# Narrowing steps moved from the first tiles of one MoE layer to its later tiles, and a regrouped preparation of the next layer

## The chip, the cores and the metric

The kernel runs on one core of a Trainium2 chip. The metric is device time in microseconds, the median of three runs. All matrix products are fp32, done as fp32r products of a high and a low part.

## The reference

Attention with mixing over heads feeds two feed-forward layers, over 1792 tokens of width 768:

```
scores = scale * q @ k^T, mixed over heads by w_pre; softmax; mixed by w_post; @ v
h  = x @ w_in            # 768 -> 1024   (first MoE)
sm = softmax(h);  solu = h * sm;  ln = (solu - mean) / sqrt(var + 1e-6) * g_ln
x2 = ln @ w_out          # 1024 -> 768
h  = x2 @ w_in2;  g = relu(h)**2;  y = g @ w_out2    # 768 -> 2048 -> 768  (second MoE)
```

The weights arrive as 64-bit floats, and the kernel narrows them to fp32 itself.

## The kernel before, in words

Three stages follow each other: attention, the first MoE and the second MoE. The code is in the order in which each engine executes it (the order is written by hand; each engine is in order, and waits on semaphores).

**First MoE.** 14 tiles of 128 tokens, `m` = 0 to 13. Tile m: `h1(m)` is 36 matmuls (L457) into `ps_h`, of which there are two; `norm1(m)` reduces (L711, VectorE), exponentiates (L714, ScalarE), multiplies and takes statistics (L715 to L722, VectorE), takes the root (L724, L725, GpSimd), and, in its second part, `nb` (L728, VectorE) and the normalised `e` (L731, ScalarE). `zt(m-1)` transposes `e` of the tile before on TensorE (L746) into `ps_tr`, and splits it (L748 ScalarE, L749 VectorE). `split_x` prepares x of tile m+2 (L700 ScalarE, L701 GpSimd). In tiles 0 to 3 two pieces each of the output weights are loaded (L681) and split (L686 ScalarE, L687 GpSimd); x and these weights share three load buffers. `out1` (L760, copied by L768, stored by L769) is 24 matmuls for one 128-row block of a group of three tiles; from tile 4 on two run per tile, ten stand after the last tile's loop.

**Narrowing.** `w2stream` narrows the second layer's weights, 96 pieces of 128x256, one piece after another: load (L789, SP queue), square on ScalarE (L799), mask on GpSimd (L800), and three integer steps on VectorE (L820, L824, L826), then a store (L807, SP queue). The mask of the next piece is asked for ahead of the first step of a piece. Each call of `next` is one step. In the first MoE `steps2` is called four times per tile, with five buffers each for raw and narrowed pieces; in the second MoE a second stream narrows the rest with three buffers each.

**Second MoE.** Products go by Strassen's scheme: seven products `p1` to `p7` per slice, 16 slices `q` (eight per half of the tokens). `prepare()` makes the sums of x (`mix_x`) and of weights (`mix_w`), and their splits (`split_xc`, `split_ti`), interleaved with the last nine `out1`. In a slice the products of q alternate with seven output blocks `y2(q-1, ·)` (L1154), in the order `SEQ`; VectorE and ScalarE read the products out of four PSUM banks (L1115 to L1131, L1101 to L1103, L1098), and `y` out of two (L1163, L1165). `mix_second()` makes the sums of x for the second half of the tokens.

Of the kernel before, what the change touches and what calls it, by code (L numbers as in the profile page):

```python
# [18 lines left out]
def kernel(  # L19
# [16 lines left out]
    nc = tc.nc  # L36
    B, D, _ = qT.shape
# [100 lines left out]
    for b in range(B):  # L138
        for (i0, n) in CHUNKS:
            c, oa = len(chunks), 0  # L140
# [593 lines left out]
    GT = 3  # L734
# [36 lines left out]
    FE = 256  # L771
    NE = F2 // FE
    KE = FE // 128
    FIRST = 60
    w2pieces = []
    for e in range(NE):
        w2pieces += [(w2_in, w2iD, c, e * FE) for c in range(CC)]
# [3 lines left out]
    def w2stream(todo, pool, nr, nt):  # L781

        raws, ts, ready = {}, {}, []

        def load(i):
            if i in todo:
                src, dst, k, o = w2pieces[i]
                raws[i] = pool.tile([128, WP], I64, tag="nraw", name="nraw", bufs=nr)
                nc.sync.dma_start(out=raws[i], in_=src[k * 128:(k + 1) * 128, o:o + WP])  # L789

        def words(i):
            pair = raws[i].bitcast(U32).rearrange("p (n two) -> p n two", two=2)
            return pair[:, :, 0], pair[:, :, 1]

        def mask(i):

            if i in todo:
                t = ts[i] = pool.tile([128, WP], F32, tag="nt", name="nt", bufs=nt)
                nc.scalar.activation(out=t, in_=words(i)[1].bitcast(F32), func=AF.Square)  # L799
                nc.gpsimd.tensor_scalar(  # L800
                    out=t, in0=t, scalar1=2.0**-30, scalar2=2.0 - 2.0**-23, op0=ALU.is_ge, op1=ALU.mult
                )

        def store():
            i = ready.pop(0)
            src, dst, k, o = w2pieces[i]
            nc.sync.dma_start(out=dst[k * 128:(k + 1) * 128, o:o + WP], in_=ts.pop(i))  # L807
            narrowed.append(i)

        a = todo[0]  # L810
        for i in range(nr - 1):
            load(a + i)
        mask(a)
        for i in todo:
            load(i + nr - 1)
            mask(i + 1)
            low, high = words(i)
            bits = ts[i].bitcast(U32)
            stt = nc.vector.scalar_tensor_tensor
            stt(out=bits, in0=high, scalar=3, in1=bits, op0=ALU.logical_shift_left, op1=ALU.bitwise_and)  # L820
            yield True
            if ready:
                store()
            stt(out=bits, in0=high, scalar=0xC0000000, in1=bits, op0=ALU.bitwise_and, op1=ALU.bitwise_or)  # L824
            yield True
            stt(out=bits, in0=low, scalar=29, in1=bits, op0=ALU.logical_shift_right, op1=ALU.bitwise_or)  # L826
            raws.pop(i)
            ready.append(i)
            yield True
        store()  # L830
        yield True

    stream = w2stream(range(FIRST), m1b_p, 5, 5)

    def steps2(n):
        for _ in range(n):
            next(stream, None)
# [4 lines left out]
    outs = []  # L842
    for m in range(NTILE):
        if m + 2 < NTILE:
            xr[m + 2] = load_x(m + 2)
        if m:
            run(h1(m))
        norm = norm1(m)
        next(norm)
        steps2(3)  # L850
        if m > 0:
            zt(m - 1)
        steps2(3)
        if m + 2 < NTILE:
            split_x(m + 2, xr.pop(m + 2))
        for kk in range(len(w1o), min(K1, len(w1o) + 2)):
            wr[kk] = load_w1_out(kk)
        for kk in sorted(wr):
            split_w1_out(kk, wr.pop(kk))
        if m > GT and (m - 1) % GT == 0:  # L860
            outs += [((m - 1) // GT - 1, cc) for cc in range(CC)]
        for i in range(2):
            if outs:
                out1(*outs.pop(0))
            steps2(4 if m else 2)
            if i == 0:
                run(norm)
    run(stream)
# [20 lines left out]
    def load_xb(p, c):  # L889
        t0 = 2 * p * HT  # L890
        qs = []
        for k in range(2):
            for t in range(2):
                b = wi2_p.tile([128, HT], F32, tag=f"xb{k}{t}", name="xb", bufs=2)
                r0 = (k * HC + c) * 128
                nc.sync.dma_start(out=b, in_=x2D[r0:r0 + 128, t0 + t * HT:t0 + (t + 1) * HT])
                qs.append(b)
        return qs

    def mix_x(qs, i, eng):  # L900

        b11, b12, b21, b22 = qs
        out, x, y = ((b11, b12, b11), (b12, b22, b12), (b22, b22, b11), (b21, b21, b22))[i]
        eng.tensor_tensor(out=out, in0=x, in1=y, op=ALU.subtract)
# [3 lines left out]
    def store_xt(p, c, name, b):  # L908
        r0 = (XT.index(name) * HC + c) * 128
        nc.sync.dma_start(out=xtD[p][r0:r0 + 128], in_=b)  # L910

    def mix_second():

        parts = [load_xb(1, 0), load_xb(1, 1)]
        yield True
        for c in range(HC):
            b11, b12, b21, b22 = qs = parts[c]
            for i in range(4):
                mix_x(qs, i, nc.gpsimd)
                if i % 2:  # L920
                    yield True
            for name, b in zip(XT, (b11, b22, b12, b21)):
                store_xt(1, c, name, b)
            if c + 2 < HC:
                parts.append(load_xb(1, c + 2))
            yield True
# [31 lines left out]
    def load_ra(q):  # L958
        if q < NQ:
            f0 = (q % NE) * FE  # L960
            for k in range(2):
                t = wi2_p.tile([128, HC, FE], F32, tag=f"ra{k}", name="ra", bufs=1)
                nc.sync.dma_start(
                    out=t,
                    in_=w2iD[k * HC * 128:(k + 1) * HC * 128, f0:f0 + FE].rearrange("(c p) f -> p c f", p=128),
                )
                ra[q, k] = t
# [51 lines left out]

    def prepare():  # L1020

        load_ra(0)
        parts = [load_xb(0, 0), load_xb(0, 1)]
        yield True
        mix_w(0, 0)
        mix_w(0, 1)
        weights = list(ORDER)
        for c in range(HC):
            b11, b12, b21, b22 = qs = parts[c]
            split_xc(0, "p1", c, b11)  # L1030
            yield True
            mix_x(qs, 0, nc.vector)
            mix_x(qs, 1, nc.vector)
            split_xc(0, "p5", c, b11)
            yield True
            mix_x(qs, 2, nc.vector)
            mix_x(qs, 3, nc.vector)
            split_xc(0, "p7", c, b12)
            yield True
            split_xc(0, "p6", c, b22)  # L1040
            store_xt(0, c, "p4", b21)
            if c + 2 < HC:
                parts.append(load_xb(0, c + 2))
            split_ti(0, weights.pop(0))
            yield True
            split_ti(0, weights.pop(0))
            yield True
        while weights:
            split_ti(0, weights.pop(0))
            yield True  # L1050

    prep2 = prepare()
    for g, cc in outs:
        for _ in range(3):
            next(prep2, None)
        out1(g, cc)
    run(prep2)
    load_xc(0, ORDER[4])
    load_ra(1)

    ps1.__exit__(None, None, None)
    psi.__exit__(None, None, None)
# [144 lines left out]
    for q in range(NQ):  # L1207
        p, e = divmod(q, NE)
        todo = []
        if q == 0:  # L1210
            todo = [(0, name) for name in ORDER[4:]]
        elif q == NE - 1:
            todo = [(1, name) for name in ORDER[:4]]
            load_xc(*todo[0])
            load_xc(*todo[1])
        elif q == NE:
            todo = [(1, name) for name in ORDER[4:]]
        parts = [(t, c) for t in todo for c in range(HC)]
        for k, x in enumerate(SEQ):
            if isinstance(x, str):  # L1220
                prod(q, x)
                after(q, x)
            elif q:
                y2(q - 1, x)
            lows()
            extras(q, k)
            for t, c in parts[:3 if q == 0 else 1]:
                if q == NE - 1 and SEQ.index(t[1]) > k:
                    break
                parts.pop(0)  # L1230
                split_xc(*t, c)
                i = ORDER.index(t[1]) + (2 if t[0] else 1)
                if c == HC - 1 and i < len(ORDER):
                    load_xc(t[0], ORDER[i])
            if p == 0:
                steps2(2 if q and k < 10 else 1)
                if 2 <= q < NE - 1 and k in (2, 6, 10):
                    next(mx, None)
        assert not parts, q
        if q < NE:  # L1240
            assert len(narrowed) >= min(12 * (q + 2) + 6, len(w2pieces)), (q, len(narrowed))
# [61 lines left out]
```

## Time and profile before

| | |
|---|---|
| median of 3 runs | 1207.66 us (1196.8 to 1211.68) |
| the profiled execution | 1203.72 us, its span 1201.9 us |
| TensorE matmul busy | 1059.8 us, 88% |
| VectorE, GpSimd, ScalarE busy | 722.9, 712.9, 581.3 us |
| TensorE's waits in the first MoE for `e` (L731) | 37.2 us in 4 |
| first MoE's last `out1` ends, second MoE begins | 698.2 us |

TensorE is the engine with most work, so a microsecond counts where TensorE waits. The profile's idle column says what ended each wait, and the timeline says when the product groups start.

### The profile page before, as it was taken

To read this page: it belongs to the slowest core of one execution; us is meant where nothing else is said; L and a number is where in the kernel's file an instruction comes from. 1 tells how busy PE (TensorE), PEld (TensorE's weight loads), DVE (VectorE), ACT (ScalarE), POOL (GpSimd) and SP (SyncE) were. 2 spreads that over 40 slices of the span, in tenths; PEclk is the share of its full clock that TensorE was granted. 3 is DMA by queue.
4 is the path that set the end of the run, shared out by engine and by line. 5 is a ranking of instruction groups with operands and counts; after the bars stand their busy time and mean duration, and the time that the engine had idled before them with its cause. 6 is when DMAs were issued, how large, how long until landed. Compare 5 with 4: busy or idle time off the path is not lost.

```text
span 1201.9 us, 30983 instructions
## 1 busy us (share of the span) xinstructions
PE 1059.8 (88%) x12488; PEld 894.5 (74%) x12488; DVE 722.9 (60%) x1262; ACT 581.3 (48%) x1212; POOL 712.9 (59%) x876
## 2 busy tenths in 40 slices
PE   8888789889998855899999848878899999999998
PEld 3555557555666744799889847877799899999998
DVE  3557676666856346686775627677764672444444
ACT  4666566667766133334333424544344556434432
POOL 3556886896848355554452427798775555555521
PEclk9999999999999867899999978998899999999999
DMA  6786786877766343554542544545521552111102
GB/s 180 205 237 197 213 252 201 257 229 225 220 190 188 105 152 118 158 151 147 163 139 81 176 165 138 158 153 182 171 94 64 168 188 82 58 62 53 53 27 92
DMA packets 128910, 183.08 MB, mean 152 GB/s; under 512 B 24416, under 2 KB 101344, under 8 KB 128768
## 3 DMA queue, kind: packets, MB, share of 16 engines
q1 hardware_dynamic: 119924, 156.59, 41.9%
q0 software_dynamic: 6464, 22.60, 6.6%
q10 hardware_dynamic: 2380, 1.93, 0.6%
q8 instruction: 98, 1.61, 0.6%
q14 instruction: 44, 0.36, 0.1%
HBM read 103.70 MB, written 38.83 MB: 119 GB/s over the span
## 4 chain that ended last, share of the span: by engine, by line
PE 63%; DVE 9%; DMA 8%; issue 7%; ACT 6%; POOL 6%; SPq 1%; ACTq 0%; POOLq 0%; DVEq 0%
PE ps_y L1154 14%; PE ps_h L1085 11%; PE ps_o L760 8%; PE ps_h L457 7%; PE ps_ring L297 6%; PE ps_ring L336 6%; PE ps_pre L240 5%; PE ps_ring L206 5%; DMA sdst<-ssrc 3%; POOL nt L800 2%; DVE nt L820 2%; DVE nt L824 1%; ACT ssrc L213 1%; POOL s L994 1%; DVE gt L1098 1%
## 5 line engine op out<-in xcount | busy, mean ns | idle before, releaser
L1154 PE MATMUL ps_y<-to,gt 128*128 128x384 f32 x1332 | 250.9, 342 | 19.7 <-DVE y L1165 15.6
L1154 PEld LDWEIGHTS ps_y<-to,gt 128*128 128x128 f32 x1332 | 238.3, 192 | 26.7 <-issue 11.8
L1085 PE MATMUL ps_h<-xc,ti 128*128 128x448 f32 x1008 | 220.9, 371 | 25.4 <-DVE h L1120 16.1
L1085 PEld LDWEIGHTS ps_h<-xc,ti 128*128 128x128 f32 x1008 | 190.4, 190 | 43.2 <-ACT ti L1009 16.5
L297 PEld LDWEIGHTS ps_ring<-w,e 60*64 60x64 f32 (+1 forms) x5760 | 104.1, 138 | 74.9 <-issue 47.2
L316 DVE COPY at<-ps_ring 128x420 f32<-128x420 f32 x156 | 87.8, 610 | 107.5 <-PE ps_ring L297 107.4
L800 POOL TENSOR_SCALAR nt<-nt 128x256 f32<-128x256 f32 x96 | 111.8, 1164 | 67.1 <-ACT nt L799 60.5
L297 PE MATMUL ps_ring<-w,e 60*64 60x60 f32 (+2 forms) x5760 | 113.0, 222 | 35.8 <-issue 28.7
L213 ACT COPY ssrc<-ps_ring 128x896 f32<-128x896 f32 x92 | 82.5, 907 | 107.8 <-PE ps_ring L206 91.6
L457 PE MATMUL ps_h<-w1i,xs 128*128 128x512 f32 x504 | 126.9, 412 | 0.0
L1165 DVE TENSOR_TENSOR y<-ps_y,y 128x768 f32<-128x768 f32 x97 | 92.2, 953 | 56.7 <-PE ps_y L1154 56.6
L760 PE MATMUL ps_o<-zt,w1o 128*128 128x384 f32 (+1 forms) x720 | 122.0, 328 | 4.0 <-ACT o L768 4.0
L760 PEld LDWEIGHTS ps_o<-zt,w1o 128*128 128x128 f32 x720 | 118.2, 190 | 4.7 <-ACT o L768 4.7
L258 ACT ACTIVATE e<-ps_pre,nm 128x448 f32<-128x448 f32 x180 | 113.3, 640 | 15.4 <-DVE nm L251 12.4
L457 PEld LDWEIGHTS ps_h<-w1i,xs 128*128 128x128 f32 x504 | 99.3, 199 | 23.0
L1098 DVE TENSOR_TENSOR gt<-h,gt 128x448 fp32r<-128x448 f32 x64 | 53.9, 842 | 94.6 <-ACT gt L1103 94.4
L251 DVE TENSOR_REDUCE nm<-ps_pre 128x1 f32<-128x448 f32 x180 | 103.1, 610 | 11.4 <-PE ps_pre L240 11.4
L206 PE MATMUL ps_ring<-k,q 64*64 64x448 f32 x752 | 102.1, 555 | 7.4 <-ACT ssrc L213 3.7
L1010 POOL TENSOR_TENSOR ti<-s,ti 128x384 fp32r<-128x384 f32 x64 | 70.7, 1115 | 53.3 <-ACT ti L1009 52.4
L240 PE MATMUL ps_pre<-sdst,wpre_bd 64*64 64x448 f32 x720 | 98.2, 563 | 4.0 <-issue 2.5
L336 PEld LDWEIGHTS ps_ring<-at,v 128*64 128x64 f32 x1536 | 76.2, 140 | 26.8 <-PE ps_pre L240 11.3
L820 DVE SCALAR_TENSOR_TENSOR nt<-nraw,nt 128x256 uint32<-128x256 uint32 x96 | 55.3, 576 | 66.7 <-POOL nt L800 66.7
(106 smaller groups left out, 1562.5 us busy)
## 6 DMA issues: line engine op xcount, KB each, us to landing
sdst<-ssrc SPq DMA_DIRECT2D x166, 210.0 KB
nraw<-in_moe_w_in_dram SPq DMA_DIRECT2D x48, 256.0 KB
nraw<-in_moe_w_out_dram SPq DMA_DIRECT2D x48, 256.0 KB
ra<-w2iD SPq DMA_DIRECT2D x32, 384.0 KB
ro<-w2oD SPq DMA_DIRECT2D x32, 384.0 KB
w1raw<-in_moe_w_in_dram POOLq DMA_DIRECT2D x24, 256.0 KB, 6.3
w1raw<-in_moe_w_out_dram POOLq DMA_DIRECT2D x24, 256.0 KB, 5.4
w2iD<-nt SPq DMA_DIRECT2D x48, 128.0 KB
```

Source lines behind the costliest of these rows:

```text
L206: nc.tensor.matmul(out=ps[64 * u:64 * u + 64, e, 0:S], lhsT=qq[c][64 * e:64 * e + 64, p * n + u * half:p * n + u * half + 64], rhs=k[64 * ...
L213: (nc.vector.tensor_copy if dve else nc.scalar.copy)(ssrc[c][:, p:H:HP, :], ps[:, :, 0:S])
L240: nc.tensor.matmul(out=ps[b][64 * u:64 * u + 64, 0:S], lhsT=wpre_bd[64 * r:64 * r + m], rhs=ds[b][64 * r:64 * r + m], start=True, stop=True,)
L251: nc.vector.tensor_reduce(out=nm, in_=pres[s][b][:, 0:S], op=ALU.max, axis=AX.X, negate=True)
L258: nc.scalar.activation(out=e, in_=pres[s][b][:, 0:S], func=AF.Exp, bias=nms.pop((s, b)), scale=1.0, accum_out=sms[s][:, b:b + 1])
L297: nc.tensor.matmul(out=ps[64 * c:64 * c + 64, u, i0:i0 + ng * RH], lhsT=e[64 * u:64 * u + m, o:o + 64], rhs=w[64 * u:64 * u + m, b, g0:g0 ...
L336: nc.tensor.matmul(out=ps[64 * e:64 * e + 64, 0, q * 120:q * 120 + n], lhsT=t[:, g] if j < NJ else t[:, e, p], rhs=at[c][:, j * H + (g if ...
L457: nc.tensor.matmul(out=ps[:, u], lhsT=t[:, a, cc], rhs=w1i[cc][:, w, u * 512:(u + 1) * 512], start=(cc == 0 and a == 0 and w == 0), stop=( ...
L760: nc.tensor.matmul(out=ps[:, 0:width], lhsT=w1o[k][:, w, cc * 128:(cc + 1) * 128], rhs=zT[:, a, k, 0:width], start=(k == 0 and i == 0), st ...
L800: nc.gpsimd.tensor_scalar(out=t, in0=t, scalar1=2.0**-30, scalar2=2.0 - 2.0**-23, op0=ALU.is_ge, op1=ALU.mult)
L1085: nc.tensor.matmul(out=bank[b][:, 0:HT], lhsT=t[:, w, c], rhs=xc[name][:, a, c], start=(first and c == 0 and i == 0), stop=(c == HC - 1 an ...
L1154: nc.tensor.matmul(out=ps[:, u - u2[0], 0:DM // 2], lhsT=gt[:, a, f, o:o + 128], rhs=w[:, v, f, u * (DM // 2):(u + 1) * (DM // 2)], start= ...
```

## The change

The order of TensorE's instructions is as before. Four things differ.

1. 72 of the 96 pieces, not 60, are narrowed in the first MoE, and the steps are given out by `rate(m, n)`: none in tiles 0 to 2, two per call in tile 3 (8), and 6, 5, 5, 5 per call from tile 4 on (21 per tile instead of 14). The stream's first step now only issues loads.
2. `prepare()` loads `p1`'s parts of x separately, splits them first, and makes the sums of a group (`mixes`) one or two chunks before their splits (`splits`). The loads for `p3` and for the next weights move into it. It runs one chunk before each of the first three `out1` and two before the others, instead of three.
3. In the second MoE the remaining 24 pieces take no step in slice 0 (one at its end), and 16 steps per slice from slice 1 on (24 before).
4. The sums of `mix_second` are on VectorE instead of GpSimd, and in slices 5 and 6 instead of 2 to 6.

```diff
-    FIRST = 60
+    FIRST = 72
...
             load(a + i)
+        yield True
         mask(a)
...
+    def rate(m, n):
+        return n if m > GT else 2 if m == GT else 0
+
...
-        steps2(3)
+        steps2(rate(m, 6))
         if m > 0:
             zt(m - 1)
-        steps2(3)
+        steps2(rate(m, 5))
...
-            steps2(4 if m else 2)
+            steps2(rate(m, 5))
             if i == 0:
                 run(norm)
...
-                mix_x(qs, i, nc.gpsimd)
+                mix_x(qs, i, nc.vector)
...
     def prepare():
 
+        load_xc(0, "p1")
+        parts = [load_xb(0, 0), load_xb(0, 1)]
         load_ra(0)
-        parts = [load_xb(0, 0), load_xb(0, 1)]
-        yield True
-        mix_w(0, 0)
-        mix_w(0, 1)
+        yield True
+        def mixes(c):
+            for i in range(4):
+                mix_x(parts[c], i, nc.vector)
+        def splits(c):
+            b11, b12, b21, b22 = parts[c]
+            store_xt(0, c, "p4", b21)
+            for name, b in (("p6", b22), ("p5", b11), ("p7", b12)):
+                split_xc(0, name, c, b)
+            if c + 2 < HC:
+                parts.append(load_xb(0, c + 2))
...
     prep2 = prepare()
-    for g, cc in outs:
-        for _ in range(3):
+    next(prep2)
+    for i, (g, cc) in enumerate(outs):
+        for _ in range(1 if i < 3 else 2):
             next(prep2, None)
         out1(g, cc)
     run(prep2)
-    load_xc(0, ORDER[4])
-    load_ra(1)
...
-                steps2(2 if q and k < 10 else 1)
-                if 2 <= q < NE - 1 and k in (2, 6, 10):
+                steps2((1 if k == 13 else 0) if q == 0 else 1 + (k in (2, 6)))
+                if NE - 3 <= q < NE - 1 and k % 2:
                     next(mx, None)
```

Where it moves instructions, at three places (the changed code's line numbers are a few higher: L820, L824, L826, L956, L1117, L1120 become L821, L825, L827, L960, L1137, L1140).

The SP queue at the start of the first MoE, before: `xraw` is x of a tile, `w1oraw` output weights, `nraw` a piece to narrow, `w2iD<-nt` the store of a narrowed piece.

```order
L693 DMA xraw<-xD 128x6x128
L789 DMA nraw<-in_moe_w_in_dram 128x256 x6
L807 DMA w2iD<-nt 128x256
L681 DMA w1oraw<-w1oD 128x768 x2
L789 DMA nraw<-in_moe_w_out_dram 128x256
L807 DMA w2iD<-nt 128x256
```

And with the change:

```order
L693 DMA xraw<-xD 128x6x128
L681 DMA w1oraw<-w1oD 128x768 x2
L693 DMA xraw<-xD 128x6x128
L681 DMA w1oraw<-w1oD 128x768 x2
L693 DMA xraw<-xD 128x6x128
L681 DMA w1oraw<-w1oD 128x768 x2
L693 DMA xraw<-xD 128x6x128
L789 DMA nraw<-in_moe_w_in_dram 128x256 x5
```

The output weights' loads no longer stand behind loads and stores of narrowed pieces.

ScalarE in a later tile of the first MoE (tile 5), before: `nt<-nraw` is the square of a piece, `e` L714 the exponent and L731 the normalised tile, `o` a copy of an output block.

```order
L714 ACTIVATE e,sm<-ps_h,nm 128x1024
L799 ACTIVATE nt<-nraw 128x256
L748 CAST zt<-ps_tr 128x4x128 x2
L799 ACTIVATE nt<-nraw 128x256
L700 CAST xs<-xraw 128x768
L768 COPY o_8299<-ps_o 128x384
L799 ACTIVATE nt<-nraw 128x256 x2
L731 ACTIVATE e<-e,nb,rs 128x1024
L768 COPY o_8345<-ps_o 128x384
L799 ACTIVATE nt<-nraw 128x256
```

And with the change:

```order
L714 ACTIVATE e,sm<-ps_h,nm 128x1024
L799 ACTIVATE nt<-nraw 128x256 x2
L748 CAST zt<-ps_tr 128x4x128 x2
L799 ACTIVATE nt<-nraw 128x256
L700 CAST xs<-xraw 128x768
L768 COPY o_8200<-ps_o 128x384
L799 ACTIVATE nt<-nraw 128x256 x2
L731 ACTIVATE e<-e,nb,rs 128x1024
L768 COPY o_8248<-ps_o 128x384
L799 ACTIVATE nt<-nraw 128x256 x2
```

Seven squares per tile stand there in every later tile, two of them behind `e`.

VectorE in slice 0 of the second MoE, before: `xc<-xr` are splits of the parts of x for p3, p2 and p4; `u` and `h` read p6 and p5.

```order
L956 TENSOR_TENSOR xc<-xr,xc 128x448 x3
L820 SCALAR_TENSOR_TENSOR nt<-nraw,nt 128x256
L1117 TENSOR_TENSOR u<-ps_h_10151,u 128x448
L956 TENSOR_TENSOR xc<-xr,xc 128x448 x3
L824 SCALAR_TENSOR_TENSOR nt<-nraw,nt 128x256
L956 TENSOR_TENSOR xc<-xr,xc 128x448 x3
L826 SCALAR_TENSOR_TENSOR nt<-nraw,nt 128x256
L1120 TENSOR_TENSOR h<-ps_h_10184,u 128x448
```

And with the change:

```order
L960 TENSOR_TENSOR xc<-xr,xc 128x448 x3
L1137 TENSOR_TENSOR u<-ps_h_10252,u 128x448
L960 TENSOR_TENSOR xc<-xr,xc 128x448 x6
L1140 TENSOR_TENSOR h<-ps_h_10283,u 128x448
L1142 TENSOR_TENSOR h<-ps_h_10306,h 128x448
```

The steps of a piece no longer stand between the splits and the reads; the nine splits are still ahead of the read of p5.

## Rows read from the trace of the kernel before

**Rows 1.** TensorE's waits: for whom, us in total, times, longest.
```profile
PE ps_tr L746 <- ACT e L731: 37.2, 4, 12.3
...
PE ps_o L760 <- ACT o L768: 4.0, 3, 1.7
```

**Rows 2.** Two stretches: length, busy time of PE, PEld, DVE, ACT, POOL, clock, DMA.
```profile
440.00:460.00 20.00, 11.90 (x44) 9.51 (x44) 11.57 (x23) 7.00 (x12) 10.27 (x9) 0.74 0.49 150
760.00:800.00 40.00, 33.41 (x174) 30.75 (x173) 28.28 (x43) 17.54 (x35) 32.52 (x26) 1.00 0.54 175
```

**Rows 3.** Timeline of TensorE, first MoE: start, length in us, what, idle before.
```profile
405.15 11.17 PE L457 MATMUL ps_h<-w1i,xs 128*128 128x512 f32 x48
...
500.36 8.54 PE L457 MATMUL ps_h<-w1i,xs 128*128 128x512 f32 x36
508.74 1.03 PE L746 MATMUL ps_tr<-id_sb,e 128*128 128x128 f32 x8
509.53 8.57 PE L760 MATMUL ps_o<-zt,w1o 128*128 128x384 f32 x48
517.94 8.55 PE L457 MATMUL ps_h<-w1i,xs 128*128 128x512 f32 x36
```

**Rows 4.** What ScalarE's split of the output weights (L686) waited for: us, times.
```profile
  DMA w1oraw<-w1oD: 37.5, 5
```

**Rows 5.** Timeline of VectorE in one later tile of the first MoE.
```profile
526.52 1.23 DVE L711 TENSOR_REDUCE nm<-ps_h 128x1 f32<-128x1024 f32 x1 [2.34 <-PE ps_h L457]
...
532.16 0.37 DVE L826 SCALAR_TENSOR_TENSOR nt<-nraw,nt 128x256 uint32<-128x256 uint32 x1
...
534.45 0.42 DVE L826 SCALAR_TENSOR_TENSOR nt<-nraw,nt 128x256 uint32<-128x256 uint32 x1
...
535.90 2.12 DVE L826 SCALAR_TENSOR_TENSOR nt<-nraw,nt 128x256 uint32<-128x256 uint32 x1
...
539.39 0.15 DVE L728 SCALAR_TENSOR_TENSOR nb<-mv,rs 128x1 f32<-128x1 f32 x1
...
542.76 0.43 DVE L820 SCALAR_TENSOR_TENSOR nt<-nraw,nt 128x256 uint32<-128x256 uint32 x1 [1.97 <-POOL nt L800]
```

**Rows 6.** Timeline of ScalarE, same tile.
```profile
539.63 1.25 ACT L731 ACTIVATE e<-e,nb,rs 128x1024 f32<-128x1024 f32 x1 [5.96 <-DVE nb L728]
```

**Rows 7.** Timeline of GpSimd, same tile.
```profile
533.38 2.42 POOL L800 TENSOR_SCALAR nt<-nt 128x256 f32<-128x256 f32 x2
535.89 1.85 POOL L701 TENSOR_TENSOR xs<-xraw,xs 128x768 fp32r<-128x768 f32 x1
```

**Rows 8.** TensorE: slices 0, 1, 5 begin; last three rows: p2 of slices 6, 7, 8.
```profile
698.15 7.59 PE L1085 MATMUL ps_h<-xc,ti 128*128 128x448 f32 x36
721.86 7.43 PE L1085 MATMUL ps_h<-xc,ti 128*128 128x448 f32 x27 [16.11 <-DVE h L1120]
732.86 5.25 PE L1085 MATMUL ps_h<-xc,ti 128*128 128x448 f32 x18 [3.57 <-ACT h L1101]
...
877.17 3.97 PE L1085 MATMUL ps_h<-xc,ti 128*128 128x448 f32 x18 [0.81 <-ACT h L1101]
...
928.66 7.50 PE L1085 MATMUL ps_h<-xc,ti 128*128 128x448 f32 x36
958.99 7.50 PE L1085 MATMUL ps_h<-xc,ti 128*128 128x448 f32 x36
...
986.51 7.50 PE L1085 MATMUL ps_h<-xc,ti 128*128 128x448 f32 x36
```

**Rows 9.** Timeline of ScalarE in slice 0.
```profile
711.85 0.43 ACT L799 ACTIVATE nt<-nraw 128x256 f32<-128x256 f32 x1 [6.86 <-DMA nraw<-in_moe_w_in_dram]
...
717.60 1.11 ACT L955 CAST xc<-xr 128x448 fp32r<-128x448 f32 x2 [3.30 <-DMA xr<-xtD]
```

**Rows 10.** Timeline of the SP queue in slice 0.
```profile
714.99 2.19 SPq L945 DMA_DIRECT2D xr<-xtD  x3
```

**Rows 11.** ScalarE's squares of pieces, 760 to 880 us: busy, mean ns, idle before, released by.
```profile
L799 ACT ACTIVATE nt<-nraw 128x256 f32<-128x256 f32 x25 | 10.9, 436 | 33.0 <-DMA w2oD<-nt 18.7 <-DMA w2iD<-nt 13.3 <-DVE h L1122 1.0
```

More of the change, by code (lines that the diff above doesn't have):

```diff
@@ L1020, in prepare @@
     def prepare():
+        load_xc(0, "p1")
+        parts = [load_xb(0, 0), load_xb(0, 1)]
         load_ra(0)
-        parts = [load_xb(0, 0), load_xb(0, 1)]
         yield True
-        mix_w(0, 0)
-        mix_w(0, 1)
+        def mixes(c):
[8 more added lines that the diff above has]
+                parts.append(load_xb(0, c + 2))
         weights = list(ORDER)
         for c in range(HC):
-            b11, b12, b21, b22 = qs = parts[c]
-            split_xc(0, "p1", c, b11)
-            yield True
[L1032 to L1044, printed above, removed]
+            split_xc(0, "p1", c)
+        yield True
+        mixes(0)
+        mix_w(0, 0)
+        yield True
+        mixes(1)
+        mix_w(0, 1)
+        yield True
+        splits(0)
+        split_ti(0, weights.pop(0))
+        yield True
+        split_ti(0, weights.pop(0))
+        yield True
+        splits(1)
+        split_ti(0, weights.pop(0))
+        yield True
+        mixes(2)
+        yield True
+        split_ti(0, weights.pop(0))
+        yield True
+        splits(2)
+        load_xc(0, ORDER[4])
+        while weights:
             yield True
             split_ti(0, weights.pop(0))
[L1047 to L1050, printed above, removed]
+        load_ra(1)
+        yield True
     prep2 = prepare()
-    for g, cc in outs:
-        for _ in range(3):
+    next(prep2)
+    for i, (g, cc) in enumerate(outs):
+        for _ in range(1 if i < 3 else 2):
             next(prep2, None)
```

## The prediction

> **What bounds the kernel now.** TensorE is busy for 88% of the span and its order of work does not change, so the time can only move where it waits or runs slowly. I read the waits of TensorE first. The largest entry is the transposes of the first MoE's early tiles, which wait for the normalised tile e: 37.2 us in only four waits [rows 1]. The reader should see that it is few and long: one cause per tile, in tiles 0 to 3. Around them the granted clock is 0.74 [rows 2], so the half-rate level for about half of the time; TensorE had idled just before each fall. Next I took TensorE's timeline for the length of whole stages, so that waits and slow clock are counted together. From the end of tile 1's products (405.15 + 11.17 = 416.3) to the start of tile 5's (500.36) it is 84.0 us; in a later tile the transposes to `out1` take 0.79, two `out1` 8.41, the products of the next tile 8.38, together 17.58 [rows 3]. Then the timelines at the border and in the slices: slice 0 takes 34.7 us, slices 1 to 4 together 144.3, a quiet slice (8) 27.5 [rows 8].
>
> **Early tiles.** What ends ScalarE's waits there is the load of the output weights, 37.5 us in five [rows 4], and e stands behind those splits on ScalarE. On the SP queue these loads stand behind loads and stores of pieces, and a store waits for VectorE's steps, which stand behind the statistics of the same tile. The change takes all of that out of tiles 0 to 2, and puts five loads ahead in tile 3. Without it e is ready as soon as its own chain allows: from the reduce to the end of the statistics 5.6 us (526.52 to 532.16); from there to nb 7.2 (to 539.39), of which ten steps of 0.42 and a stretch of 1.7 fall away and 1.3 remain for the root and the splits of the transposes [rows 5]; and 1.5 to the end of e [rows 6]. That is 8.5 to 9 us, against 0.8 + 8.4 of TensorE work in between. The stage then is 4 x 0.79 + 3 x 8.38 + 8.41 = 36.7 us. I add 2 for late buffers of the output weights in tile 1 and for the five piece loads in tile 3. Gain 84.0 - 38.7 = **45.3**. Bounds: 47.3 if nothing waits; 28.7 if half of the 37.2 us of waits stays.
>
> **Later tiles.** Here the work goes. In the row's tile ten steps of 0.42 stood between the statistics (532.16) and nb (539.39), one of them stretched to 2.12 us beside GpSimd's split of x [rows 5, 7]. Now sixteen steps stand there: nb comes 5.64 + 7.23 + 6 x 0.42 = 15.4 us after the reduce, and e is complete 1.5 later, at 16.9. That is inside the period of 17.58. But behind nb stand five steps, and the last is the first of a piece whose square stands behind e on ScalarE. The row has this very wait: nb at 539.39, e at 539.63, the step at 542.76 to 543.19 [rows 5, 6], so 3.8 us after nb. Before, VectorE had idle time for it; now the next reduce queues behind it, at 15.4 + 3.8 = 19.2 us, against 17.6 of TensorE. So the lag grows by 1.6 per tile. e of tile 5 comes 0.9 late (19.2 + 16.9 against 2 x 17.58); of tiles 6 to 11 1.6 each (9.7); tile 12 has no x to split and is not late; tile 13, where only the transposes and three `out1` stand between (13.4 us), is late by about 4.1. Loss **14.7**. Bounds: 0, if that wait vanishes (VectorE's sum is then 15.4 + 5 x 0.42 = 17.5), and 30, if each tile waits for a second square as well.
>
> Against a row, one rule. A step that runs beside GpSimd's mask is not longer: 0.42 at 534.45, inside the masks of 533.38 to 535.80; only the two-input split of x stretches one [rows 5, 7]. The Trainium skill's "SBUF — State Buffer" (Who interferes with whom) says that a VectorE instruction with two SBUF inputs contends with a GpSimd instruction that reads SBUF, and that the second to issue fully blocks. By that rule the seven masks of a tile would block steps too; the split of x agrees with it, the masks do not.
>
> **The border.** The three waits of the last `out1` for ScalarE's copies, 4.0 us [rows 1], come from splits that stand ahead of the copies and wait for VectorE's sums; these now come a chunk earlier. I take **2.7** of them (0 to 4). In slice 0 the first 36 products end 7.6 us after its start, and p3 waits until 23.7 (721.86 - 698.15) for VectorE's read of p5 [rows 8]. VectorE had a step ahead of it, whose square waited 6.9 us for its piece [rows 9]; that is gone. What is left is the chain of x parts: p3's are loaded already, so ScalarE splits them after its copy of p1 (2.6 after the start) and VectorE ends at 4.9; p2's loads go out as buffers fall free, and land 2.6 us later, as 714.99 to 717.60 for p4's [rows 9, 10], so p2's splits end at about 9.0; p4's the same way at 12.9. p3 starts at 13.6, 10.1 earlier. Of the 11.0 us from there to slice 1 (7.43 for 27 products, 3.57 of wait) I take 2 off. Slice 0 gains **12.1** (bounds 6 and 18).
>
> **Slices 1 to 4.** 144.3 us against 4 x 27.52 = 110.1: an excess of 34.2 [rows 8]. In these slices ScalarE's squares sat idle for 33.0 us, all but 1 for the stores that free one of three buffers [rows 11]; VectorE's step waits for the mask, and its reads of products and y stand behind the step. With 16 steps a piece takes about 5 us instead of 3.4, so the buffer is back in time, and GpSimd loses the sums of x. Bounds: nothing left of the excess; or 16/24 of it, 22.8. The nearest row is slice 7, where twelve further splits on VectorE and ScalarE cost 30.33 - 27.52 = 2.8 us [rows 8]; I take 2 per slice. Gain 34.2 - 8 = **26.2**. The new wait there is the first step of slice 1, whose piece is loaded only at the end of slice 0; some 9 us, hidden while TensorE has 11 us of products and two free y buffers.
>
> **Slices 5 and 6** get nine steps and twelve sums on VectorE: 21 operations at slice 7's price for 12, 2.8, would be 4.9; I take **4** (0 to 8).
>
> **Sum**, against the profiled execution: 1203.7 - 45.3 + 14.7 - 2.7 - 12.1 - 26.2 + 4.0 = **1136** us. That execution is 3.9 below the median of the runs (1207.7), within their spread, and I leave the forecast there.
>
> **Rivals.** (a) *GpSimd bounds the second MoE.* It was busy for 32.5 of 40 us at 760 to 800 [rows 2], and sums, splits and masks remain on it; then slices 1 to 4 gain only 34.2 - 22.8 = 11.4, slice 0 only 6, slices 5 and 6 lose 8: 1203.7 - 45.3 + 14.7 - 2.7 - 6 - 11.4 + 8 = 1161. For it: the steps' waits there end with masks. Against: the masks themselves waited for ScalarE, and ScalarE for stores. (b) *The masks block VectorE in the later tiles.* Five masks of 1.2 us per tile meet steps (two are waited for anyway): 6 us more for each of nine tiles, 54: 1190, within 2% of before. The 0.42 us step inside a mask speaks against it. By the rule of the Trainium skill named above ("SBUF — State Buffer") this is what would happen. (c) *Slower: the narrowing chain of the later tiles waits for its stores.* In the row of the second MoE 33.0 us of idle stand before 25 squares, 1.3 us each [rows 11]. With seven pieces a tile, each passing ScalarE, store and buffer in line, that is 9 us more per tile, and if TensorE waits with it, nine tiles cost 83, and the clock falls as at 440 to 460, which makes the 8.4 us of products some 1.6 longer, 15 more: 1136 + 98 = 1234. It decides from 8 us per tile on (72 over nine). Against: five buffers instead of three, and in the tile's row the squares run ahead of the masks.
>
> **Chances.** Forecast with its bounds 0.78, (a) 0.12, (b) 0.06, (c) 0.04. This kernel's measurement can tell about 2%, 24 us, from no change. The forecast's errors side by side (early tiles -2 to +17, later tiles -15 to +15, border 8 and 6 to either side, slices 1 to 4 -8 to +15) seldom add; I take 1111 to 1167, which takes in (a). Faster by over 2% are the forecast and (a), less a little: 0.89; within 2% (b) and a remainder, 0.07; slower 0.04.
>
> **What would show it.** In the profile after: the four waits of the transposes for e shrink to a few us, and the clock reads 1.00 from 420 on; from tile 5 to 11 a wait of 1 to 2 us per tile appears before the transposes, released by e, and VectorE idles less than 1 us per tile but for the mask behind e; p3 of slice 0 starts about 14 us after p1, behind the splits of p4; slices 1 to 4 take 28 to 30 us. I am wrong if the tiles' wait is over 4 us or absent, if ScalarE's splits of the output weights still wait over 5 us per tile, or if slices 1 to 4 stay above 32 us.

## The result and the profile after

The changed kernel takes **1157.78 us** (median; 1148.75 to 1165.32), the kernel before, beside it on the same chip, 1204.26 us: a ratio of 0.961, 95% interval 0.952 to 0.971. The forecast was 1136 us, its range 1111 to 1167. So the kernel is faster, inside the range, by two thirds of what the sum said. (Of the version with p4's splits behind p7, further down, the profiled execution was a slower one, 1166.13 us against 1147.94 to 1158.44, and its ratio is of the other three.)

First the page of the changed kernel: busy time of each engine, share of the span, instructions.

```profile
PE 1054.2 (91%) x12488; PEld 888.2 (77%) x12488; DVE 722.9 (62%) x1274; ACT 581.1 (50%) x1212; POOL 696.2 (60%) x864
```

VectorE is busy for 722.9 us as before, but not with the same work: twelve sums of x came to it from GpSimd (L908 21.7 us, where L904 had 10.2), and the 288 narrowing steps take 158.7 us instead of 173.9. What matters is the change in TensorE's idle time. Where it is now, by TensorE's waits (for whom, us in total, times, longest):

```profile
PE ps_tr L746 <- ACT e L731: 23.7, 11, 7.3
PE ps_y L1174 <- DVE y L1185: 13.8, 10, 5.1
```

Against [rows 1] the wait for e has lost 13.5 us of 37.2, but it is another wait now: eleven of them, one of 7.3 us. To price the terms one by one, take TensorE's timeline of the changed kernel at the marks between the stages (start, length, what, idle before it):

```profile
406.43 11.17 PE L457 MATMUL ps_h<-w1i,xs 128*128 128x512 f32 x48
...
455.34 1.97 PE L746 MATMUL ps_tr<-id_sb,e 128*128 128x128 f32 x8 [7.25 <-ACT e L731]
456.95 9.67 PE L760 MATMUL ps_o<-zt,w1o 128*128 128x384 f32 x48
466.46 8.55 PE L457 MATMUL ps_h<-w1i,xs 128*128 128x512 f32 x36
...
550.64 1.09 PE L746 MATMUL ps_tr<-id_sb,e 128*128 128x128 f32 x8 [1.62 <-ACT e L731]
...
644.84 1.97 PE L746 MATMUL ps_tr<-id_sb,e 128*128 128x128 f32 x8 [4.30 <-ACT e L731]
...
674.85 6.01 PE L760 MATMUL ps_o<-zt,w1o 128*128 128x256 f32 x48 [2.30 <-ACT o L768]
680.70 7.59 PE L1105 MATMUL ps_h<-xc,ti 128*128 128x448 f32 x36
695.97 12.01 PE L1105 MATMUL ps_h<-xc,ti 128*128 128x448 f32 x45 [7.67 <-ACT ti L1013]
707.82 2.27 PE L1174 MATMUL ps_y<-to,gt 128*128 128x384 f32 x12
...
828.54 2.24 PE L1174 MATMUL ps_y<-to,gt 128*128 128x384 f32 x12
...
843.84 4.18 PE L1174 MATMUL ps_y<-to,gt 128*128 128x384 f32 x12 [5.13 <-DVE y L1185]
...
864.36 2.27 PE L1174 MATMUL ps_y<-to,gt 128*128 128x384 f32 x12
...
891.88 2.27 PE L1174 MATMUL ps_y<-to,gt 128*128 128x384 f32 x12
```

The mark of a slice is here its first block of y, because slice 0's p4 and slice 1's p1 and p6 stand in one row. The same marks of the kernel before that [rows 3, 8] don't hold (last transposes, first y of slices 1, 5, 7):

```profile
662.77 1.03 PE L746 MATMUL ps_tr<-id_sb,e 128*128 128x128 f32 x8
...
737.94 2.25 PE L1154 MATMUL ps_y<-to,gt 128*128 128x384 f32 x12
...
880.98 2.25 PE L1154 MATMUL ps_y<-to,gt 128*128 128x384 f32 x12
...
936.00 2.27 PE L1154 MATMUL ps_y<-to,gt 128*128 128x384 f32 x12
```

| stage (marks) | before | predicted | after |
|---|---|---|---|
| early tiles: end of tile 1's products to start of tile 5's | 84.0 | 38.7 | 48.9 |
| later tiles: to the last transposes | 162.4 | 177.1 | 178.4 |
| last `out1`: to slice 0 | 35.4 | 32.7 | 35.9 |
| slice 0: to the first y of slice 1 | 39.8 | 27.7 | 27.1 |
| slices 1 to 4 | 143.0 | 116.8 | 120.7 |
| slices 5 and 6 | 55.0 | 59.0 | 63.3 |

The gain is 45.3 us between these marks, against 67.6 by the terms. Ten of the missing 22 lie in the early tiles, the rest in the last `out1` (3.2), slices 1 to 4 (3.9), slices 5 and 6 (4.3) and the later tiles (1.3); slice 0 gained 0.6 more than forecast.

**Tile 3.** VectorE of the changed kernel between the statistics of tile 3 and nb (L728), and the next reduce:

```profile
443.62 0.21 DVE L722 BATCH_NORM_AGGREGATE mv<-st 128x2 f32<-128x12 f32 x1
445.93 0.43 DVE L821 SCALAR_TENSOR_TENSOR nt<-nraw,nt 128x256 uint32<-128x256 uint32 x1 [2.10 <-POOL nt L800]
...
447.47 2.00 DVE L825 SCALAR_TENSOR_TENSOR nt<-nraw,nt 128x256 uint32<-128x256 uint32 x1
449.50 1.91 DVE L827 SCALAR_TENSOR_TENSOR nt<-nraw,nt 128x256 uint32<-128x256 uint32 x1
451.33 2.02 DVE L821 SCALAR_TENSOR_TENSOR nt<-nraw,nt 128x256 uint32<-128x256 uint32 x1
453.38 0.50 DVE L825 SCALAR_TENSOR_TENSOR nt<-nraw,nt 128x256 uint32<-128x256 uint32 x1
453.80 0.15 DVE L728 SCALAR_TENSOR_TENSOR nb<-mv,rs 128x1 f32<-128x1 f32 x1
```

and GpSimd in the same stretch:

```profile
444.80 2.48 POOL L800 TENSOR_SCALAR nt<-nt 128x256 f32<-128x256 f32 x2
447.37 1.82 POOL L701 TENSOR_TENSOR xs<-xraw,xs 128x768 fp32r<-128x768 f32 x1
449.14 3.92 POOL L687 TENSOR_TENSOR w1o<-w1oraw,w1o 128x768 fp32r<-128x768 f32 x2
```

The step inside the masks takes 0.43; the three beside the two-input splits of x and of the output weights take 1.9 to 2.0, and each ends some 0.3 us behind one of those splits. Of the 10.2 us from the statistics to nb, 2.1 are a wait for the mask, which stood behind the root (L724, L725) on GpSimd, and some 4.7 the stretching.

**Later tiles.** VectorE and ScalarE of the changed kernel around nb of one later tile:

```profile
549.10 0.15 DVE L728 SCALAR_TENSOR_TENSOR nb<-mv,rs 128x1 f32<-128x1 f32 x1
...
552.48 0.43 DVE L821 SCALAR_TENSOR_TENSOR nt<-nraw,nt 128x256 uint32<-128x256 uint32 x1 [1.58 <-POOL nt L800]
552.82 1.22 DVE L711 TENSOR_REDUCE nm<-ps_h 128x1 f32<-128x1024 f32 x1
```

```profile
549.35 1.24 ACT L731 ACTIVATE e<-e,nb,rs 128x1024 f32<-128x1024 f32 x1 [3.43 <-DVE nb L728]
...
550.86 0.77 ACT L799 ACTIVATE nt<-nraw 128x256 f32<-128x256 f32 x2
```

This is the chain of the forecast: nb, e, a square behind e, its mask, the step 3.4 us after nb, and at once the reduce.

### The profile page after: what moved, and what is told of

Read it like the earlier page. It is cut to its first block, busy times and chain, and to the rows that moved or that the text cites. A ratio compares the mean times of both kernels' runs of the same rounds, so it can differ in the third digit from the quotient of the medians.

```text
span 1157.5 us, 30995 instructions
## 1 busy us (share of the span) xinstructions
PE 1054.2 (91%) x12488; PEld 888.2 (77%) x12488; DVE 722.9 (62%) x1274; ACT 581.1 (50%) x1212; POOL 696.2 (60%) x864
## 4 chain that ended last, share of the span: by engine, by line
PE 51%; DVE 12%; DMA 10%; POOL 9%; issue 9%; ACT 6%; SPq 2%; POOLq 0%; ACTq 0%; DVEq 0%
PE ps_y L1174 13%; PE ps_h L1105 11%; PE ps_ring L297 6%; PE ps_ring L336 6%; PE ps_pre L240 5%; PE ps_ring L206 4%; PE ps_h L457 4%; DMA sdst<-ssrc 3%; POOL nt L800 3%; PE ps_o L760 2%; DMA w2oD<-nt 2%; DMA w2iD<-nt 2%; DVE nt L825 2%; DVE nt L821 2%; POOL ti L1014 1%
## 5 line engine op out<-in xcount | busy, mean ns | idle before, releaser
L1174 PE MATMUL ps_y<-to,gt 128*128 128x384 f32 x1332 | 246.8, 338 | 15.7 <-DVE y L1185 13.8
L1174 PEld LDWEIGHTS ps_y<-to,gt 128*128 128x128 f32 x1332 | 234.6, 189 | 22.1 <-DVE y L1185 8.8
L1185 DVE TENSOR_TENSOR y<-ps_y,y 128x768 f32<-128x768 f32 x97 | 92.1, 953 | 52.9 <-PE ps_y L1174 52.9
L457 PE MATMUL ps_h<-w1i,xs 128*128 128x512 f32 x504 | 121.2, 399 | 0.0
L457 PEld LDWEIGHTS ps_h<-w1i,xs 128*128 128x128 f32 x504 | 95.0, 190 | 21.5
L1118 DVE TENSOR_TENSOR gt<-h,gt 128x448 fp32r<-128x448 f32 x64 | 51.0, 797 | 95.2 <-ACT gt L1123 95.1
L336 PE MATMUL ps_ring<-at,v 128*64 128x120 f32 (+1 forms) x1536 | 84.3, 268 | 6.0 <-ACT ssrc L213 5.5
```

Source lines behind the costliest of these rows:

```text
L336: nc.tensor.matmul(out=ps[64 * e:64 * e + 64, 0, q * 120:q * 120 + n], lhsT=t[:, g] if j < NJ else t[:, e, p], rhs=at[c][:, j * H + (g if ...
L457: nc.tensor.matmul(out=ps[:, u], lhsT=t[:, a, cc], rhs=w1i[cc][:, w, u * 512:(u + 1) * 512], start=(cc == 0 and a == 0 and w == 0), stop=( ...
L1174: nc.tensor.matmul(out=ps[:, u - u2[0], 0:DM // 2], lhsT=gt[:, a, f, o:o + 128], rhs=w[:, v, f, u * (DM // 2):(u + 1) * (DM // 2)], start= ...
L1185: nc.vector.tensor_tensor(out=yo, in0=po, in1=yo, op=ALU.add)
```

## The experiments

The attention part is the same in all of these kernels, yet tile 1's products end anywhere from 414.4 to 426.9 us after the start. So whole times of two kernels a few us apart say little, and each verdict goes by the stretch between the marks above, in one profiled execution of each kernel. Where the code of a stage is as in the change, these executions differ by 0.8 us in the early tiles, 1.1 in the later ones, 1.8 in the last `out1` and 0.6 in slice 0; a smaller difference shows nothing.

**Tile 3's steps behind nb** (`GT` is 3).

```
-        return n if m > GT else 2 if m == GT else 0
+        return n if m > GT else 0
...
-        steps2(rate(m, 6))
+        steps2(1 if m == GT else rate(m, 6))
...
-            steps2(rate(m, 5))
+            steps2(7 if m == GT and i else rate(m, 5))
```

> Tile 3 still issues its five loads of pieces where it did, but its seven arithmetic steps stand behind nb instead of six of them ahead of it. Theory (the steps, stretched to 1.9 to 2.1 us beside GpSimd's two-input splits, hold up nb): the transposes of tile 3 wait under 1.5 us instead of 7.25, and the stretch from tile 1's products to tile 5's falls from 48.9 to 40 to 41.5 us (the wait and some 2.4 us of slow clock behind it); whole kernel 6 to 9 us less. Rival 1 (the loads on the SP queue make ScalarE's splits of the output weights late): the wait stays above 4 us. Rival 2 (the steps now hold up tile 4's reduce): the wait moves to the transposes of tile 4, 2 to 5 us there.

1159.67 us, ratio to before 0.961 (0.958 to 0.964), as the change, where 6 to 9 us less were expected. TensorE at the transposes of tiles 3 and 4:

```profile
450.77 1.09 PE L746 MATMUL ps_tr<-id_sb,e 128*128 128x128 f32 x8 [0.70 <-ACT e L731]
...
473.94 1.97 PE L746 MATMUL ps_tr<-id_sb,e 128*128 128x128 f32 x8 [5.36 <-ACT e L731]
```

The theory is right on the cause: the loads stayed where they were, and the wait of tile 3 fell from 7.25 to 0.70, the early stretch to 40.4. But rival 2 happened too: the seven steps first waited 5.0 us for squares and masks, which stood behind `e` on ScalarE and behind the splits of the output weights on GpSimd; tile 4's reduce stood behind these steps, and its transposes waited 5.36. The delay was moved on by one tile, and the start of tile 6's products gained 0.7 us.

**Masks two pieces ahead.**

```
-        mask(a)
+        for i in range(ahead):
+            mask(a + i)
...
-            mask(i + 1)
+            mask(i + ahead)
...
-    stream = w2stream(range(FIRST), m1b_p, 5, 5)
+    stream = w2stream(range(FIRST), m1b_p, 5, 5, 2)
```

> In the first MoE the mask of a piece is asked for two pieces ahead instead of one. Theory (the last step behind nb waits for a mask whose square stands behind e on ScalarE): the waits of 1.6 us before the transposes of six tiles vanish or fall under 0.4, the 4.3 of the last tile falls to 1 to 2.5, the stretch from tile 5's products to the last transposes falls from 178.4 to 165 to 168 us, the last out1s by about 1 more; whole kernel 10 to 14 us less. Rival (VectorE's own work of about 17.5 us per tile, with stretched steps, sets the 19.4 us period): waits and stretch change by less than 3 us.

1146.8 us, ratio 0.950 (0.946 to 0.955). The stretch of the later tiles is 164.6 us instead of 178.4. Two periods of TensorE in it:

```profile
541.00 8.54 PE L457 MATMUL ps_h<-w1i,xs 128*128 128x512 f32 x36
549.39 1.03 PE L746 MATMUL ps_tr<-id_sb,e 128*128 128x128 f32 x8
...
558.58 8.55 PE L457 MATMUL ps_h<-w1i,xs 128*128 128x512 f32 x36
```

17.58 us, TensorE's own time [rows 3], with the same 21 steps per tile. The mask behind e was 13.8 of the 16.0 us lost; the rival is out. No wait for e is left in these tiles; most of the rest is a new wait for a copy, between the three `out1` of the last tile:

```profile
630.70 4.46 PE L760 MATMUL ps_o<-zt,w1o 128*128 128x384 f32 x24 [1.62 <-ACT o L768]
```

The last `out1` did not follow: 37.3 us, with a wait of 4.03 for a copy.

**Early loads for the second half's sums.**

```
-                if NE - 3 <= q < NE - 1 and k % 2:
+                if NE - 3 <= q < NE - 1 and k % 2 or (q, k) == (NE - 4, 11):
```

> The eight loads for the second half's sums are issued at the end of slice 4 instead of early in slice 5, and every sum comes two positions sooner. Theory (VectorE waits 2.3 us for these loads with the read of y behind it): TensorE's wait of 5.1 us in slice 5 falls to 3 or less, and slice 5 from 35.8 to 31 to 33.5 us, as the slow clock behind the wait goes too. Rival (the sums themselves, 1.28 us each beside GpSimd, are the cost): the wait moves with them and slice 5 stays above 34.5.

1153.25 us, ratio 0.956 (0.952 to 0.959). In the changed kernel VectorE waits for the loads, then makes two sums, and the read of y (L1185) stands behind them:

```profile
840.27 2.56 DVE L908 TENSOR_TENSOR xb<-xb 128x448 f32<-128x448 f32 x2 [2.31 <-DMA xb<-x2D]
842.75 0.94 DVE L1185 TENSOR_TENSOR y<-ps_y,y 128x768 f32<-128x768 f32 x1
```

With early loads the wait of 5.13 becomes three of 0.96 to 1.45, and slice 5 takes 31.8 us (827.28 to 859.06) instead of 35.8, as expected. The 4.3 us that it still takes over a quiet slice are of steps and sums together.

**The same sums on GpSimd.**

```
-                mix_x(qs, i, nc.vector)
+                mix_x(qs, i, nc.gpsimd)
```

> The sums of the second half go back to GpSimd, at the places that they have in the change (slices 5 and 6). Theory (VectorE's wait for their loads, and the sums of 1.28 us, hold the read of y): the wait of 5.1 us in slice 5 goes, slices 5 and 6 take 56 to 59 us instead of 63.3. Rival (GpSimd has no room for them beside its splits and masks): steps and splits come late instead, and slices 5 and 6 stay at 62 us or more.

1155.24 us, ratio 0.959 (0.953 to 0.964). Slices 5 and 6 take 61.3 us: between the two expectations. The wait of 5.13 is gone, so VectorE's queue was the place; a new wait of 2.1 us for GpSimd's split of the output weights says that the rival is partly right too.

**p4's splits behind p7, in slice 0.**

```
-            for t, c in parts[:3 if q == 0 else 1]:
+            for t, c in parts[:(3 if k in (0, 1, 5) else 0) if q == 0 else 1]:
```

> In slice 0 p4's three splits come behind p7's products instead of ahead of the read of p5. Theory (the read of p5 stands on VectorE behind p4's splits, and these behind their loads): p3 starts 10 to 11.5 us after p1 instead of 15.3, the wait of 7.7 falls to 2.5 to 4, slice 0 takes 22.5 to 24 us instead of 27.1. Rival 1 (VectorE is held by p2's splits and GpSimd's sums): p3 starts 13.5 or later. Rival 2 (p4's splits now hold up the read of p3 and what follows): p3 is early, but slice 0 still takes over 26 us.

1156.07 us, ratio 0.956 (0.951 to 0.961). p3 starts 10.5 us after p1 (692.08), and slice 0 takes 23.6 us; the wait is now named after the read of p5 itself:

```profile
702.61 8.54 PE L1105 MATMUL ps_h<-xc,ti 128*128 128x448 f32 x27 [2.94 <-DVE h L1140]
```

Rival 1 and rival 2 are out. So the chain of part loads that the forecast priced was the bound, and one of its three links need not stand there.

**24 steps per slice again.**

```
-                steps2((1 if k == 13 else 0) if q == 0 else 1 + (k in (2, 6)))
+                steps2((1 if k == 13 else 0) if q == 0 else 1 + (k < 10))
```

> The narrowing steps of the second MoE go back to 24 per slice; there are as many pieces as in the change, so they end in slice 4. Theory (the rate is what costs: a third buffer is not back in time): slices 1 to 3 take 33 to 36 us each, slice 4 28, together 128 to 136 us for slices 1 to 4 instead of 120.7. Rival (each step costs the same at any rate, or the gain of slices 1 to 4 came from the sums that left GpSimd): 119 to 123 together.

1164.01 us, ratio 0.967 (0.960 to 0.974). First y of slices 4, 5 and 7 (slice 1's is at 714.01):

```profile
816.47 2.25 PE L1174 MATMUL ps_y<-to,gt 128*128 128x384 f32 x12
...
843.97 2.27 PE L1174 MATMUL ps_y<-to,gt 128*128 128x384 f32 x12
...
899.93 2.27 PE L1174 MATMUL ps_y<-to,gt 128*128 128x384 f32 x12
```

Slices 1 to 3 take 34.2 us each, slice 4, with two steps left, 27.5; together 130.0, as the theory said. A slice costs 27.5 without steps, 30.2 with 16 and 34.2 with 24: the last eight cost 4.0, the first sixteen 2.7. What I had not thought of: slices 5 and 6, free of steps, take 56.0 us with the very sums that cost the change 63.3.

**Steps spread over all tiles.**

```
-        return n if m > GT else 2 if m == GT else 0
+        return 4 if m else 2
```

> The narrowing steps are spread over all tiles again (four per call, two in tile 0), with the same 72 pieces; the rest is as in the change. Theory (loads and stores of pieces ahead of the output weights' loads, and steps ahead of nb, are what makes e late in the early tiles): the stretch from tile 1's products to tile 5's is 78 to 92 us instead of 48.9, and the later tiles, with 16 steps instead of 21, take 158 to 166 instead of 178.4: 12 to 28 us slower than the change. Rival (the early tiles' gain came from elsewhere, the border of attention or the clock): under 65 us in the early stretch.

1184.79 us, ratio 0.983 (0.975 to 0.991). Against the kernel before that is too little to call it faster by 2%. Early stretch 85.9, later tiles 162.7 us, as the theory had them. ScalarE's wait for the output weights (L686) in this kernel, and in the change:

```profile
  DMA w1oraw<-w1oD: 34.5, 6
```

```profile
  DMA w1oraw<-w1oD: 3.6, 3
```

So the early gain comes from where the steps stand, and between the marks it is worth some 21 us: 37.0 in the early stretch, less 15.7 in the later tiles (the medians differ by 27).

**Four buffers for out1's copies.**

```
-        o = m1_p.tile([128, GT * 128], F32, tag="o", name="o1", bufs=2)
+        o = m1_p.tile([128, GT * 128], F32, tag="o", name="o1", bufs=4)
```

> The copies of out1 get four buffers instead of two. Theory (in the last out1s ScalarE's copy waits 4.0 us for a store that stands behind the loads of x and weights, and splits and sums follow from there): that wait goes, TensorE's wait of 2.3 us falls under 0.7, and the stretch from the last transposes to slice 0 falls from 35.9 to 33 to 34.5 us. Rival (the splits stand ahead of the copies and wait for VectorE's sums, 5.4 us): TensorE still waits over 1.5 us and the stretch stays above 35.

1158.7 us, ratio 0.961 (0.956 to 0.967). ScalarE no longer waits for the store, but TensorE's wait is 2.34 and the stretch 35.5 us: the theory falls. What holds the copies is VectorE, here in the changed kernel:

```profile
652.23 0.63 DVE L960 TENSOR_TENSOR xc<-xr,xc 128x448 fp32r<-128x448 f32 x1 [0.61 <-ACT xc L959]
...
662.44 7.88 DVE L960 TENSOR_TENSOR xc<-xb,xc 128x448 fp32r<-128x448 f32 x6 [1.59 <-ACT xc L959]
670.25 3.41 DVE L908 TENSOR_TENSOR xb<-xb 128x448 f32<-128x448 f32 x4
```

and ScalarE, whose split waits for these sums with the copy (L768) behind it:

```profile
673.03 1.50 ACT L959 CAST xc<-xb 128x448 fp32r<-128x448 f32 x3 [5.37 <-DVE xb L908]
674.43 0.36 ACT L768 COPY o<-ps_o 128x256 f32<-128x256 f32 x1
```

Six splits take 1.31 us each, beside GpSimd's sums and splits of weights; a lone one takes 0.63.

**Four changes together, and no steps ahead of tile 4.** Masks two ahead, early loads, p4 late, and in `prepare` the splits of the third group behind one more split of weights:

```
         split_ti(0, weights.pop(0))
         yield True
+        split_ti(0, weights.pop(0))
+        yield True
         splits(2)
```

> Together: masks two pieces ahead in the first MoE, the early loads for the second half's sums, p4's splits behind p7, and in the last out1s the splits of the third group one weight split later, so that the copy of one more out1 stands ahead of them. Theory: each removes its own wait: early stretch 48, later tiles 164.6, last out1s 33 to 34.5 (the wait of 2.3 or 4.0 for the copy under 1: VectorE's sums, not stores, held that copy), slice 0 23.6, slices 1 to 4 120.5, slices 5 and 6 59.3: some 449 us from tile 1's products to slice 7 instead of 474. Rival (a wait removed comes back at the next place, as with tile 3's steps): 458 or more. If the copies are held by something else, the last out1s stay at 35 or more.

1136.87 us, ratio 0.943 (0.939 to 0.948). From tile 1's products to slice 7 453.7 us instead of 474.3, between the theory's 449 and the rival's 458. The stages of the table: 48.1, 166.7, 33.4, 24.5, 121.4, 59.7. The last `out1` are 3.9 us shorter than with the masks alone; their waits are now two, of 0.98 and 1.02. The second version also starts the steps in tile 4, with two pieces fewer (`FIRST = 70`):

> The same, and no arithmetic step of the narrowing ahead of tile 4 (tile 3 only issues the loads, as its last act); 70 pieces in the first MoE instead of 72. Theory (VectorE has no idle time in the later tiles, so a delay in tile 3 or 4 can only be avoided, not made up): the transposes of tiles 3 and 4 wait under 1.5 us each, the early stretch takes 40 to 41.5 us and the later tiles 164 to 167; some 440 us from tile 1's products to slice 7. Rival (the first steps of tile 4 wait for their loads, squares and masks and hold nb): 3 us or more of wait in tile 4, and the time of the version with 72 pieces.

1138.2 us, ratio 0.944 (0.940 to 0.948). The early stretch is 39.5 us and tile 4 waits 1.86, as the theory has it. But slices 5 and 6 took some 66 us, which I put down to its six more steps in the second MoE: they fall into slice 5, beside the sums (not tried apart). And the whole (452.6 us to slice 7) is that of the version before.

**Sums behind the last steps; tile 3's steps at the end.** As the version with 72 pieces and four changes, but with this line in place of the early loads; it is shown against the change:

```
-                if NE - 3 <= q < NE - 1 and k % 2:
+                if q == NE - 3 and k in (5, 9, 11, 13) or q == NE - 2 and k % 2:
```

> As the version with 72 pieces and four changes together, but the sums for the second half begin behind the last narrowing steps of slice 5 (loads at its fifth position, first sums at its ninth) instead of earlier. Theory (in slice 5 steps and sums share VectorE, each alone fits: with all steps done by slice 4, slices 5 and 6 took 56.0 us with the same sums): slices 5 and 6 take 55.5 to 57.5 us instead of 59.7, and from tile 1's products to slice 7 some 451 instead of 453.7. Rival (the sums, packed closer into slice 6, hold its reads of y): slice 6 takes over 29.5 and the two together 59 or more.

1136.6 us, ratio 0.942 (0.939 to 0.945). Slices 5 and 6 take 57.2 us instead of 59.7, and it is 449.0 to slice 7. But the stretch ends too early: slice 7 took 33.3 us instead of 29.6, with a wait that was not there:

```profile
876.41 9.33 PE L1177 MATMUL ps_y<-to,gt 128*128 128x384 f32 x36 [2.71 <-DVE y L1188]
```

Slices 5 to 7 together take 90.5 us, against 89.2 with the four changes and 88.4 in the version that follows, which has the same late sums: what slices 5 and 6 gained came back in slice 7, and a gain of the late sums is not shown. The last version takes the same sums, and moves tile 3's steps:

```
-        return n if m > GT else 2 if m == GT else 0
+        return n + (3 if (m, n) == (12, 6) else 0) if m > GT else 0
...
-            steps2(rate(m, 5))
+            steps2(rate(m, 5) + (i and {GT: 1, 13: 4}.get(m, 0)))
```

> The same, and tile 3 only issues loads of pieces; its seven steps go to tile 12 (three) and to tile 13 behind nb (four), whose tiles have no x to split and no next reduce behind them. Theory (a delay ahead of tile 4 is carried through all later tiles; steps at the end cost little): early stretch 39.5 to 41 us, later tiles 165 to 168, last out1s 33.5 to 36, slices 5 and 6 55.5 to 57.5: some 443 us from tile 1's products to slice 7, and 6 to 9 us less than the version beside it. Rival (the steps at the end hold up the sums of the border): last out1s and slice 0 grow by 4 us or more and the gain is under 4.

**1129.42 us**, ratio 0.9375 (0.934 to 0.941): 7 us less than the version beside it, and below the change, whose ratio is 0.961. Early stretch 39.8, later tiles 168.2, last `out1` 33.0, slice 0 24.2, 443.2 to slice 7. TensorE at tiles 3 and 4:

```profile
444.90 1.09 PE L746 MATMUL ps_tr<-id_sb,e 128*128 128x128 f32 x8
...
464.14 1.09 PE L746 MATMUL ps_tr<-id_sb,e 128*128 128x128 f32 x8 [1.43 <-ACT e L731]
```

## Why the prediction was right, and where its sum was off

**Early tiles.** The cause was right: with the steps gone from tiles 0 to 2 the output weights are in time, and these tiles wait 2.25 us together. The failed step is "I add 2 for late buffers of the output weights in tile 1 and for the five piece loads in tile 3". I priced the loads of tile 3 and forgot its arithmetic: five steps ahead of nb, one behind a mask and three beside GpSimd's splits. It cost 8.4 us (48.9 against 40.4 with the steps behind nb): 6.55 of wait (7.25 against 0.70) and 1.9 of slower transposes and `out1` after it: the granted clock is 0.83 from 440 to 460, where I had said 1.00 (0.74 before [rows 2]). I had the row for it: the one step of 2.12 us [rows 5], of which tile 3 has three, since it splits weights beside x.

**Later tiles.** Forecast 14.7, measured 16.0. The lag of 1.6 us per tile was 1.58 to 1.62, six times, then 0.22 and 4.30 as worked out (nothing and 4.1); tile 5 had none of the 0.9. The waits sum to 14.2. What the sum left out is that each wait also ends an overlap: products to transposes take 8.55 besides the wait where they took 8.38 [rows 3], transposes to the next products 9.26 instead of 9.20, together 0.23 per wait, seven times.

**Last `out1`.** "I take 2.7 of them" was the wrong row to follow. The waits for copies fell from 4.0 to 2.3 us only, since VectorE's six splits in a row, at 1.31 us each beside GpSimd, hold the third group's sums and with them a copy. The store was not it, as four buffers showed, and the loads were not: the sums ahead of these splits ended at 660.85, before ScalarE began its part at 661.83. But that is 1.1 of the missing 3.2 us. The other 2.1 are the slower TensorE behind tile 13's wait of 4.30, which I had priced as a wait alone: with the waits left out, the stage took 33.6 us instead of 31.4. The granted clock just there is 0.68, so TensorE ran at the lower of its two levels for part of the time (length, busy time of the engines, clock, DMA):

```profile
640.00:650.00 10.00, 5.70 (x23) 5.38 (x22) 6.24 (x15) 3.82 (x7) 2.48 (x2) 0.68 0.58 192
```

Before, it was 1.00 in the same stage (660 to 700 us).

**Slice 0.** 12.1 forecast, 12.7 measured, and that it came out so near is luck: two errors cancel. p3 came 15.3 us after p1 where 13.6 was said, because p3's own splits took 1.3 us each beside GpSimd's sums of weights, so its start gained 8.4 us instead of 10.1; from there to the first y the slice gained 4.2 where I took 2, since the wait of 3.57 [rows 8] went. How much is owed to the steps that left slice 0, and how much to the loads that moved into `prepare()`, no run shows: they were not tried apart.

**Slices 1 to 4.** "I take 2 per slice" measured 2.7 (10.6 us for the four). That is 2.6 of the missing 3.9 us; the other 1.3 come from the mark, by which these slices took 143.0 us before and not 144.3. Slice 7's price for twelve splits was a fair guess for sixteen steps in size only. That the rate decides is shown: 16 steps 2.7, 24 steps 6.7. ScalarE's 24 squares in the changed kernel still wait 21.3 us for stores, against 32.0 for 25 of them [rows 11].

**Slices 5 and 6.** "21 operations at slice 7's price" gave 4.9, of which I took 4; it is 8.3. The work alone was not the price: sums without steps cost 0.9 us in slice 5 (28.4 against 27.5), though VectorE waited 1.9 us for their loads there too. Steps and late loads together were, in front of a read of y (5.13 of wait, and 4.18 instead of 2.3 for the products after it): early loads alone took 4.0 of the 8.3 away, no steps in slice 5 took 7.3.

**The rivals.** GpSimd did not bound slices 1 to 4 (rival a): they gained 22.3 us where it said 11.4, and lost 9.3 of them again when only the rate went back to 24. Masks do not block steps (rival b): with all seven masks per tile the later tiles ran at 17.58. The pieces' chain with five buffers keeps up (rival c): the tiles lost 1.6 us each and not 9. The Trainium skill's "SBUF — State Buffer" (Who interferes with whom) says that a two-input VectorE instruction contends with a GpSimd instruction that reads SBUF, and calls the port pair that the two engines share an exclusive lock. For two-input work on both sides the trace agrees: the three steps of tile 3 end with GpSimd's splits. For the one-input mask it doesn't: 0.43 us inside it in tile 3, and in the median of the 95 steps that lie inside masks from 466 to 644 us. Not longer at all, as the forecast had it from one row, is too strong: these 95 take 0.41 to 0.64 us, steps beside neither masks nor splits 0.37 to 0.43.

## What to carry to other kernels

When work is moved into stages that are nearly full, price the first stage that receives it by itself: its steps wait there for squares and masks that have only begun, and meet that stage's own work. A delay ahead of a full pipeline was carried through it here, not made up; it must be avoided, or put where no stage follows. And in an engine that works in order, ask of each moved step what its producer stands behind: here one mask asked for a piece earlier was worth 14 us.

## What the runs showed of the hardware

VectorE's two-input operations on SBUF lengthen from 0.42 to about 2.0 us and from 0.63 to 1.31 beside GpSimd's two-input ones, and GpSimd's sums of weights from 1.01 to 1.40 beside them; inside its one-input masks the steps stay at 0.43 in the median, 0.64 at most. In the changed kernel the transposes after waits of 1.6 us took 1.09 us, at a granted clock of 1.00 (500 to 560 us), after 4.30 and 7.25 1.97, with 0.68 and 0.83 in the stretches around them. Open is what part of the remaining 2.7 us per slice is the stores and what VectorE's own steps, and whether slice 7's wait in the version with late sums comes from the stores of the sums or from their splits: neither was tried apart.
